# A planned instruction order for a linear-attention and SwiGLU block: priorities tuned wait by wait, one product moved, six idle products and eight ordering edges added

## The chip, the cores and the metric

The kernel runs on one core of one Trainium2 chip. The metric is the device time of one execution in microseconds (us), taken as the median of several executions.

## The reference

The input x has 2048 rows of 1024 values. The reference computes, with all matrices in bf16:

```python
xn = layernorm(x)
q, k, v = split(xn @ wqkv)                 # 32 heads of 32
pq, pk = phi(q), phi(k)                    # phi(t) = (t+1 if t > 0 else exp(t)) + 1e-6
kv = einsum("bhsd,bhse->bhde", pk, v); z = pk summed over s
s = (pq @ kv / (pq . z + 1e-6)) @ wo
g = silu((silu(x @ w_gate) * (x @ w_up)) @ w_down)    # w_gate, w_up: 1024 x 3584
out = x + s * g
```

Here x in the second branch is the layernormed xn as well.

## The kernel before

**Products.** Most matrix products are cut as in Strassen's method: a 2 x 2 block product is made from seven products of sums and differences of blocks (numbered 1 to 7 in the code) instead of eight. Where the products 1 and 5 belong to two neighbouring column blocks, they are cut once more (the "joint" products, named j1a to j1d and j5a to j5d). VectorE (DVE) makes the sums of weight blocks and of data blocks, ScalarE (ACT) copies results out of the eight PSUM banks, and DVE adds intermediate sums back into a bank. A product 6 of a set is followed by such an addition (`ps <- ps, TM`), and product 7 of that set writes into the bank that the addition reads, so it has to wait for it.

**Stages.** First K and V for all 16 row tiles (each tile is normalised by `ln_tile`, turned on its side by `t_tile`, and multiplied by `p_piece` for the first two tiles, by sets for the others; `a_tile` sums up kv). `combos` (line 523) makes four differences of weight blocks for K and V in two DVE instructions each. Then two passes over half of the rows: queries, gate and up products, the attention output, and last the down projection (`down`), whose order of products is written out in the strings `IN_D`, `ON_D`, `OUT_D` and `END_D`. `OUT_D` holds for the end of the first pass alone. The mark `X` in it calls `turn_pass`, which loads the second half of the data into the arena P, makes its differences, and prepares the first query pair of the second pass.

**Order.** The text of the kernel only lists operations with what they read and write. The class `Plan` decides on the order in which each engine runs them. `place` is a list scheduler on planned costs: it walks through time and gives each engine the next operation. TensorE (PE) takes the oldest ready group among the next six of the written order (`WINDOW=6`); DVE, ACT, GpSimd (POOL) and SyncE (SP, all DMA issues but two) take the ready one with the earliest due time less its `boost`. Due times (`schedule`) are counted back from the written order of PE's work. `schedule` runs `place` 24 times; between two runs `lift` (line 138) adds 2.0 to the boost of operations that were held up on a chain that made PE wait by 0.15 or more, and the plan with the earliest end is kept. `emit` turns the plan into one instruction list for each engine with semaphore waits. Each engine then runs its list strictly in that order, so an instruction that waits holds up everything behind it on its engine.

**The start.** Two loads of x tiles and four loads of 512 KB of K weights are issued in a row. PE runs 15 warm-up products on zeros (`NWARM`), then the transposes of tile 0 (four groups of two), then the K product of tile 0, one load of weights at a time. In `ln_tile` the DVE instructions of one tile are: two statistics, one aggregation (line 744), `veps` (line 745), then POOL raises it to the power -1/2 (`rstd`, line 748), then for tiles 0 and 1 two DVE instructions normalise a half each (line 755). The list `first` holds operations of tile 0 that the statistics of tile 1 have to follow.

Of the kernel before, what the change touches and what calls it, by code (L numbers as in the profile page):

```python
# [10 lines left out]
ALU = mybir.AluOpType  # L11
# [4 lines left out]
GRAN = 256  # L16


PASSES, LIFT = 24, 2.0
TABLE, DMA_SLACK, HOLD, YIELD = 1.28, 2.0, 0.1, 10  # L20


# [12 lines left out]
class Plan:  # L35
# [71 lines left out]
    def schedule(self):  # L107
        ops = self.ops
        for o in reversed(ops):
            d = o.pecum if o.eng == "pe" else o.pecum + o.cushion  # L110
            for s in o.succs:
                extra = (4.0 + o.nbytes / 200e3) if o.sem is not None else o.busy + o.lat
                d = min(d, s.dl - extra)
            o.dl = d - o.urgent
        pes = [o for o in ops if o.eng == "pe"]
        cum = [o.pecum + o.busy for o in pes]
        for o in ops:
            if o.sem is not None and o.succs:
                k = bisect_right(cum, o.dl - self.lead) - 1
                if k >= 0 and pes[k] not in o.preds:  # L120
                    o.preds.add(pes[k])
                    pes[k].succs.append(o)
        best = None
        for n in range(PASSES):
            end = self.place()
            if best is None or end < best[0] - 0.01:
                best = (end, self.order, {o: (o.start, o.done) for o in ops})
            if n + 1 < PASSES:
                self.lift()
        self.order = best[1]  # L130
        for o, (a, b) in best[2].items():
            o.start, o.done = a, b
        return self.order

    def lift(self):

        prev, last = {}, {}
        for o in self.order:
            prev[o] = last.get(o.eng)
            last[o.eng] = o  # L140
        for o in self.order:
            p = prev[o]
            if o.eng != "pe" or p is None or o.start - p.start - p.busy < 0.15:
                continue
            c = o
            for _ in range(12):
                late = max(c.preds, key=lambda p: p.done, default=None)
                if late is None:
                    break
                if c.eng not in ("pe", "sp") and c.start - max(c.ready, late.done) > 0.02:  # L150
                    c.boost += LIFT
                c = late

    def place(self):
        ops = self.ops
        for o in ops:
            o.npred = len(o.preds) + len(o.after)
            o.ready = 0.0
        free = {e: 0.0 for e in self.ENGS}
        dma_free = 0.0  # L160
        tab = None
        avail = {e: [] for e in self.ENGS}
        pe_next = deque(o for o in ops if o.eng == "pe")
        for o in ops:
            if o.npred == 0:
                avail[o.eng].append(o)
        order = []
        done = set()
        total = len(ops)
        while len(order) < total:  # L170
            best = None
            for e in self.ENGS:
                a = avail[e]
                if not a:
                    continue
                t = free[e]
                if e == "pe":
                    lim = None
                    n = 0
                    for o in pe_next:  # L180
                        if n >= self.window:
                            lim = o.idx
                            break
                        n += 1
                    cand = [o for o in a if lim is None or o.idx < lim]
                    if not cand:
                        continue
                    rdy = [o for o in cand if o.ready <= t + 0.05]
                    o = min(rdy, key=lambda o: o.idx) if rdy else min(cand, key=lambda o: (o.ready, o.idx))
                else:  # L190
                    rdy = [o for o in a if o.ready <= t]
                    soon = [o for o in a if o.ready > t]
                    while rdy:
                        o = min(rdy, key=lambda o: (o.dl - o.boost, o.idx))
                        q = [q for q in soon if q.ready + HOLD < t + o.busy and q.dl - q.boost + YIELD < o.dl - o.boost] if e != "sp" else ()
                        if not q:
                            break
                        rdy.remove(o)
                    if not rdy:
                        o = min(soon or a, key=lambda o: (o.ready, o.dl))  # L200
                s = max(t, o.ready)
                if e == "act" and o.tab is not None and o.tab != tab:
                    s += TABLE
                if best is None or s < best[0]:
                    best = (s, e, o)
            s, e, o = best
            if o.tab is not None:
                tab = o.tab
            o.start = s
            if o.sem is not None:  # L210
                free[e] = s + o.busy
                b = max(s + 1.8, dma_free)
                dma_free = b + o.nbytes / 340e3
                o.done = dma_free + DMA_SLACK
            else:
                free[e] = s + o.busy
                o.done = s + o.busy + o.lat
            avail[e].remove(o)
            if e == "pe":
                done.add(o)  # L220
                while pe_next and pe_next[0] in done:
                    pe_next.popleft()
            order.append(o)
            for q in o.succs:
                q.npred -= 1
                q.ready = max(q.ready, s + o.busy if q.eng == o.eng and (o.eng == "pe" or o in q.after) else o.done)
                if q.npred == 0:
                    avail[q.eng].append(q)
        self.order = order
        return max(o.done for o in ops)  # L230

    def emit(self, esem):
        prog = {e: [] for e in self.ENGS}
# [55 lines left out]
def build_kernel(nc, A_x, A_wqkv, A_wo, B_w_gate, B_w_up, B_w_down, out, WINDOW=6, NWARM=15, NPE=4, LEAD=12.0):  # L289
# [12 lines left out]
    with ExitStack() as es:  # L302
# [24 lines left out]
        X = Arena("X", 28 * KB)  # L327
# [24 lines left out]
        ps = [es.enter_context(nc.psum_tensor("ps%d" % b, [128, 512], F32)) for b in range(8)]  # L352
        bank_r = [named("bank", b) for b in range(8)]
# [36 lines left out]
        PL = Plan(WINDOW, LEAD)  # L390
# [6 lines left out]
        def pe_mm(reads, writes, mms):  # L397
            return PL.op("pe", reads, writes, partial(_mm_group, mms), mm_cost(mms))
# [21 lines left out]
        def tt(reads, writes, o, a, b, op, fast=False):  # L420
            return dve(reads, writes, lambda h: h.tensor_tensor(o, a, b, op), nel(o), 1.92 if fast else 0.96)  # L421
# [98 lines left out]
                                          ("R10", PQ0 + 8 * KB), ("R11", PQ0 + 12 * KB), ("T2", RB0),  # L520
                                          ("T3", RB0 + 4 * KB), ("T4", RB0 + 8 * KB))}

        def combos(v):
            for o, a, b in (("T3", "R11", "R01"), ("T1", "R01", "R00"), ("T2", "R11", "T1"), ("T4", "R10", "T2")):
                for h in range(2):
                    w = {}
                    for nm in (o, a, b):
                        ap, r = v[nm]
                        n = len(r.keys) // 2
                        w[nm] = ap[:, 2 * h:2 * h + 2, :], Region(r.keys[n * h:n * h + n])  # L530
                    tt([w[a][1], w[b][1]], [w[o][1]], w[o][0], w[a][0], w[b][0], ALU.subtract, True)


        wz = TM.at(0, 1 * KB, FP16)
# [3 lines left out]
        for n in range(NWARM):  # L538
            b = n % 8
# [193 lines left out]
        def ln_tile(i):  # L733
# [18 lines left out]
            if i < 2:  # L752
                n = 512
                for c in range(0, 1024, n):
                    o0 = dve([s.r, mvr, rsr], [o.sub(2 * c, 2 * n).r], lambda h, c=c: h.tensor_scalar(
                        oa[:, c:c + n], xa[:, c:c + n], mv[:, j, 0:1], rstd[:, j, :], ALU.subtract, ALU.mult), n, 2.6)
                if i == 0:
                    first.append(o0)
            else:
                dve([mvr, rsr], [nmr], lambda h: h.scalar_tensor_tensor(  # L760
                    nmean[:, j, :], mv[:, j, 0:1], -1.0, rstd[:, j, :], ALU.mult, ALU.mult), 60)
                act([s.r, nmr, rsr], [o.r], oa, xa, ACT.Identity, "sb", bias=nmean[:, j, :], scale=rstd[:, j, :])
# [152 lines left out]
                o.urgent = 60.0 - 2 * n  # L915
        ln_tile(0)
        t_tile(0)
        ln_tile(1)
        p_piece(0, 0, 1)
        p_piece(0, 0, 0)  # L920
# [5 lines left out]
        ln_tile(2)  # L926
        p_piece(0, 1, 1)
        t_tile(2)
        combos(KVV[0])
        p_piece(1, 1, 1)  # L930
        ln_tile(3)
        p_piece(0, 1, 0)
# [638 lines left out]

        IN_D = "7_0 3_0 7_1 3_1 H nj1a 4_0 nj1b 4_1 nj1c n2_0p nj1d n2_0q nj5a n2_1p nj5b n2_1q nj5c n6_0 nj5d"
        ON_D = "L 7_0 K0 6_1 7_1 K1 nj1a 3_0 nj1b 3_1 S nj1c 4a nj5a nj1d 4b nj5b n2_0 nj5c n2_1 nj5d n6_0"
        OUT_D = "7_0 3_0 X 6_1 7_1 nj1a 3_1 nj1b nj1c 4a nj5a nj1d 4b nj5b n2_0 nj5c n6_0 n2_1 nj5d n6_1"
        END_D = "7_0 6_1 7_1 3_0 3_1 4_0 4_1"

        def down(p):
# [171 lines left out]
```

## Time and profile before

| what | value |
|---|---|
| median of 4 runs | 717.62 us (716.91 to 718.32) |
| profiled execution, its own time | 716.91 us |
| its span, first to last instruction | 715.2 us |
| PE busy | 707.1 us, 99% |
| DVE busy | 641.8 us, 90% |
| ACT busy | 405.5 us, 57% |
| mean granted TensorE clock | 0.999 |

A row of the timeline gives the start and the length in us, engine, line, operation, what is written and read, how many instructions are merged into the row, and in brackets the idle time before them with what ended it. PE is the matmul stream, PEld the loading of its stationary operand, which runs beside it. The end of a matmul is modelled, so two matmuls that follow each other closely overlap in such rows; the spacing of starts tells more.

### The profile page before, as it was taken

To read this page: it belongs to the slowest core of one execution; us is meant where nothing else is said; L and a number is where in the kernel's file an instruction comes from. 1 tells how busy PE (TensorE), PEld (TensorE's weight loads), DVE (VectorE), ACT (ScalarE), POOL (GpSimd) and SP (SyncE) were. 2 spreads that over 40 slices of the span, in tenths; PEclk is the share of its full clock that TensorE was granted. 3 is DMA by queue.
4 is the path that set the end of the run, shared out by engine and by line. 5 is a ranking of instruction groups with operands and counts; after the bars stand their busy time and mean duration, and the time that the engine had idled before them with its cause. 6 is when DMAs were issued, how large, how long until landed. Compare 5 with 4: busy or idle time off the path is not lost.

```text
span 715.2 us, 11264 instructions
## 1 busy us (share of the span) xinstructions
PE 707.1 (99%) x4143; PEld 389.4 (54%) x4143; DVE 641.8 (90%) x1533; ACT 405.5 (57%) x779; POOL 12.8 (2%) x35
## 2 busy tenths in 40 slices
PE   8999999999999999999999999999999999999997
PEld 3544445555555555555556455555555555565654
DVE  6999888989999999998957999999999999797863
ACT  3767654887669565654222157676886756521212
POOL 2111000000000000000000000000000000000000
PEclk9999999999999999999999999999999999999999
DMA  9425235145464343326595964132715241646653
GB/s 298 114 60 127 51 117 177 60 141 198 143 191 121 125 143 124 97 73 168 145 196 159 275 161 141 60 118 93 206 61 179 87 148 60 180 137 160 143 155 96
DMA packets 138758, 98.11 MB, mean 137 GB/s; under 512 B 32848, under 2 KB 135760, under 8 KB 138704
## 3 DMA queue, kind: packets, MB, share of 16 engines
q1 hardware_dynamic: 138416, 97.21, 47.8%
q8 instruction: 32, 0.52, 0.3%
q10 hardware_dynamic: 288, 0.20, 0.1%
q14 instruction: 22, 0.18, 0.1%
HBM read 77.59 MB, written 12.71 MB: 126 GB/s over the span
## 4 chain that ended last, share of the span: by engine, by line
PE 95%; DVE 2%; DMA 1%; ACT 0%; SPq 0%; issue 0%
PE ps L278 95%; DMA H<-in_A_wqkv_dram 1%; DVE W L421 1%; DVE H L421 1%; DVE ps L421 0%; PE ps L285 0%; DVE TM L421 0%; DVE P L421 0%; ACT TM L410 0%; SPq L424 0%; ACT ps L410 0%; DVE H L818 0%; SPq L722 0%; DVE TM L817 0%; DVE X L421 0%
## 5 line engine op out<-in xcount | busy, mean ns | idle before, releaser
L278 PE MATMUL ps<-X,W 128*128 128x512 f16 (+2 forms) x1372 | 289.2, 350 | 0.6 <-DVE W L421 0.6
L410 ACT ACTIVATE TM<-ps 128x512 f16<-128x512 f32 (+3 forms) x355 | 186.8, 548 | 108.9 <-PE ps L278 106.5
L278 PE MATMUL ps<-H,W 128*128 128x512 f16 (+2 forms) x1096 | 219.2, 351 | 0.6 <-DVE ps L421 0.4
L421 DVE TENSOR_TENSOR W<-W 128x1024 f16<-128x1024 bf16 (+5 forms) x416 | 186.4, 482 | 6.0 <-PE ps L278 5.2
L278 PEld LDWEIGHTS ps<-X,W 128*128 128x128 f16 (+1 forms) x1372 | 132.6, 98 | 105.0 <-DVE W L421 1.1
L278 PEld LDWEIGHTS ps<-H,W 128*128 128x128 f16 (+1 forms) x1096 | 105.5, 98 | 95.2 <-DVE ps L421 1.5
L421 DVE TENSOR_TENSOR ps<-ps,TM 128x256 f32<-128x256 f32 (+1 forms) x250 | 131.4, 529 | 13.2 <-PE ps L278 10.9
L410 ACT ACTIVATE ps<-ps 128x512 f32<-128x512 f32 (+1 forms) x174 | 85.1, 489 | 100.1 <-PE ps L278 98.3
L278 PE MATMUL ps<-P,W 128*128 128x256 f16 (+1 forms) x516 | 99.5, 319 | 0.1
L410 ACT ACTIVATE H<-ps 128x512 f16<-128x512 f32 (+1 forms) x126 | 75.1, 605 | 41.5 <-PE ps L278 41.3
L421 DVE TENSOR_TENSOR H<-H 128x1024 f16<-128x1024 f16 (+5 forms) x126 | 70.7, 580 | 1.3 <-DMA H<-in_A_wqkv_dram 0.8
L278 PEld LDWEIGHTS ps<-P,W 128*128 128x128 f16 (+1 forms) x516 | 50.3, 98 | 29.5 <-DVE ps L421 0.7
L410 ACT ACTIVATE TM<-TM 128x512 f16<-128x512 f32 (+1 forms) x61 | 37.9, 622 | 47.0 <-DVE TM L421 46.7
L278 PE MATMUL ps<-W 128*128 128x256 f16 (+1 forms) x330 | 62.0, 282 | 0.0
L421 DVE TENSOR_TENSOR TM<-ps,TM 128x512 f32<-128x512 f32 (+3 forms) x63 | 41.7, 662 | 13.2 <-PE ps L278 12.4
L421 DVE TENSOR_TENSOR H<-H,TM 128x512 f16<-128x512 f16 x112 | 45.6, 419 | 8.9 <-ACT H L410 8.7
L278 PEld LDWEIGHTS ps<-W 128*128 128x128 f16 (+1 forms) x330 | 31.6, 98 | 32.5 <-DVE ps L421 1.3
L278 PE MATMUL ps<-H,X 128*128 128x512 bf16 (+1 forms) x150 | 35.5, 379 | 0.8 <-DMA H<-in_A_wqkv_dram 0.8
L278 PE MATMUL ps<-H,P 128*128 128x512 bf16 (+1 forms) x110 | 26.8, 379 | 0.0
L421 DVE TENSOR_TENSOR H<-ps,TM 128x512 f16<-128x512 f32 (+1 forms) x35 | 24.0, 687 | 1.9 <-PE ps L278 1.5
L278 PEld LDWEIGHTS ps<-H,X 128*128 128x128 f16 (+1 forms) x150 | 14.0, 98 | 17.9 <-ACT X L410 1.2
L421 DVE TENSOR_TENSOR TM<-TM,W 128x512 f16<-128x512 f16 (+1 forms) x39 | 14.2, 366 | 10.5 <-ACT TM L410 10.5
(97 smaller groups left out, 431.3 us busy)
## 6 DMA issues: line engine op xcount, KB each, us to landing
W<-in_B_w_gate_dram SPq DMA_DIRECT2D x14, 1024.0 KB, 5.2
W<-in_B_w_up_dram SPq DMA_DIRECT2D x13, 1024.0 KB, 5.5
W<-in_B_w_down_dram SPq DMA_DIRECT2D x14, 896.0 KB, 6.3
H<-in_A_wqkv_dram SPq DMA_DIRECT2D x8, 512.0 KB, 8.0
H<-r_scratch SPq DMA_DIRECT2D x32, 128.0 KB, 3.6
W<-m_scratch SPq DMA_DIRECT2D x4, 1024.0 KB, 5.2
s_scratch<-TM SPq DMA_DIRECT2D x32, 128.0 KB, 2.5
TM<-in_A_x_dram SPq DMA_DIRECT2D x16, 256.0 KB, 3.4
```

Source lines behind the costliest of these rows:

```text
L278: last = h.matmul(o, l, r, start=st, stop=sp, skip_group_check=True)
L410: q = PL.op("act", reads, writes, lambda h: h.activation(o, i, func, **kw), nel(o) / (1000.0 if "bias" in kw or not isinstance(kw.get("sca ...
L421: return dve(reads, writes, lambda h: h.tensor_tensor(o, a, b, op), nel(o), 1.92 if fast else 0.96)
```

## The change

The planner's `lift` with its 24 passes goes. In its place `tune` plans once, takes the first place in order of time where PE's planned wait is over 0.1 us, collects up to 14 operations of ACT, DVE and POOL on the chain that led there which were held up by their own engine, and tries up to 24 variants: for the first one, two, three or all of them, their boost is raised, or that of the operation ahead of them lowered, by 2, 5 or 12. A variant counts by PE's planned idle time from the start up to 7 us of PE work beyond that place; the best is kept if it saves more than 0.03 us, otherwise the search goes on behind the place. `place` returns PE's idle time instead of the end, and can stop early.

Three edits change what is planned. Six products of 128 columns on zeros stand between the transposes of tile 0 and its first K product. The eight differences of K weight blocks have to follow the last normalising instruction of tile 1. In `OUT_D` product 6 of set 1 (`6_1`) stands first.

```diff
-PASSES, LIFT = 24, 2.0
+GAP, SPAN = 0.1, 7
...
-        best = None
-        for n in range(PASSES):
-            end = self.place()
...
+        self.tune()
+        self.place()
         return self.order
...
+    def tune(self):
+        self.place()
+        front = 0.0
+        while True:
+            prev, last, work, at = {}, {}, 0.0, None
+            for o in self.order:
+                p = prev[o] = last.get(o.eng)
+                last[o.eng] = o
+                if o.eng == "pe":
+                    if p is not None and work > front and o.start - p.start - p.busy > GAP:
+                        at = o
+                        break
+                    work += o.busy
+            if at is None:
+                return
+            held = []
+            c = at
+            for _ in range(14):
+                late = max(c.preds, key=lambda p: (p.done, p.idx), default=None)
+                if late is None:
+                    break
+                if c.eng in ("act", "dve", "pool") and c.start - max(c.ready, late.done) > 0.02:
+                    held.append((c, prev[c]))
+                c = late
+            base = self.place(work + SPAN)
+            best = None
+            for deep in (1, 2, 3, 14):
+                for lift in (2.0, 5.0, 12.0):
+                    for sign in (0, 1):
+                        part = held[:deep]
...
+                        for c, b in part:
+                            if sign and b is not None:
+                                b.boost -= lift
+                            else:
+                                c.boost += lift
+                        v = self.place(work + SPAN)
...
+            if best is not None and best[0] < base - 0.03:
+                for o, x in best[1]:
+                    o.boost = x
+            else:
+                front = work + 0.01
+            self.place()
...
             if e == "pe":
+                idle += s - was
+                work += o.busy
+                if work > limit:
+                    return idle
...
-        return max(o.done for o in ops)
+        return idle
...
-        def combos(v):
+        def combos(v, after=None):
...
-                    tt([w[a][1], w[b][1]], [w[o][1]], w[o][0], w[a][0], w[b][0], ALU.subtract, True)
+                    q = tt([w[a][1], w[b][1]], [w[o][1]], w[o][0], w[a][0], w[b][0], ALU.subtract, True)
+                    if after is not None:
+                        q.preds.add(after)
+                        after.succs.append(q)
...
-                if i == 0:
-                    first.append(o0)
+                first.append(o0)
...
         t_tile(0)
+        tr = [o for o in PL.ops if o.eng == "pe"][-1]
+        for n in range(6):
+            o = pe_mm(wz_r[:1], [bank_r[kvb[2]]], [(ps[kvb[2]][:, 0:128], wz[:, 0:128], wz[:, 0:128], True, True)])
+            o.preds.add(tr)
+            tr.succs.append(o)
+            o.urgent = -4.0
         ln_tile(1)
...
-        combos(KVV[0])
+        combos(KVV[0], first[-1])
...
-        OUT_D = "7_0 3_0 X 6_1 7_1 nj1a 3_1 nj1b nj1c 4a nj5a nj1d 4b nj5b n2_0 nj5c n6_0 n2_1 nj5d n6_1"
+        OUT_D = "6_1 7_0 3_0 X 7_1 nj1a 3_1 nj1b nj1c 4a nj5a nj1d 4b nj5b n2_0 nj5c n6_0 n2_1 nj5d n6_1"
```

More of the change, by code (lines that the diff above doesn't have):

```diff
@@ L122, in schedule @@
                     pes[k].succs.append(o)
-        best = None
-        for n in range(PASSES):
-            end = self.place()
[L126 to L132, printed above, removed]
-        return self.order
[L135 to L147, printed above, removed]
+        self.tune()
@@ L148, in lift @@
                 if late is None:
                     break
-                if c.eng not in ("pe", "sp") and c.start - max(c.ready, late.done) > 0.02:
-                    c.boost += LIFT
+                if c.eng in ("act", "dve", "pool") and c.start - max(c.ready, late.done) > 0.02:
+                    held.append((c, prev[c]))
                 c = late
-    def place(self):
+            base = self.place(work + SPAN)
[4 more added lines that the diff above has]
+                        part = held[:deep]
+                        if deep > 1 and len(held) < deep and deep != 14:
+                            continue
+                        old = [(o, o.boost) for c, b in part for o in (c, b) if o is not None]
+                        for c, b in part:
[4 more added lines that the diff above has]
+                        v = self.place(work + SPAN)
+                        new = [(o, o.boost) for o, _ in old]
+                        for o, x in reversed(old):
+                            o.boost = x
+                        if best is None or v < best[0]:
+                            best = (v, new)
@@ L155, in place @@
+            if best is not None and best[0] < base - 0.03:
+                for o, x in best[1]:
+                    o.boost = x
+            else:
+                front = work + 0.01
+            self.place()
+    def place(self, limit=1e9):
         ops = self.ops
+        idle = work = 0.0
         for o in ops:
@@ L209, in place @@
             o.start = s
+            was = free[e]
             if o.sem is not None:
```

## The prediction

> **What bounds the kernel now.** I read the page's busy shares first, then PE's groups by shape to count its products, then PE's timeline for spacings, then the full timeline around each hole.
>
> ```profile
> PE 707.1 (99%) x4143; PEld 389.4 (54%) x4143; DVE 641.8 (90%) x1533; ACT 405.5 (57%) x779; POOL 12.8 (2%) x35
> ```
>
> PE's busy time is modelled, so I count instead. In the row of 32 products below, each costs (7.08 - 0.38) / 31 = 0.216 us; 256 columns cost 0.109, 128 columns 0.056. The groups by shape add up to 2485, 1450 and 208 products of these widths: 536.3 + 158.3 + 11.7 = 706.3 us, less 5.0 because the 64 small products with Zh run side by side (32 of them in 0.99 us): 701.3. From PE's first product at 1.04 to its last end at 712.16 are 711.1 us. So some 9.6 us are waits, and this change can win from nothing else. By spacing they lie so: 1.4 in the warm-up, where products of 512 columns start every 0.427 us; 3.0 from there to 11.6 us (half of it before the first transpose); 3.1 in sixteen holes of 0.07 to 0.76 us in the rest; 0.8 before the very last transpose; about 1 in crumbs under 0.06.
>
> The start, from the timeline:
>
> ```profile
> 7.28 1.04 PE L278 MATMUL ps<-H,X 128*128 128x512 bf16 x4
> 7.55 0.21 DVE L744 BATCH_NORM_AGGREGATE mv<-stats 128x2 f32<-128x12 f32 x1
> 8.57 0.69 DVE L421 TENSOR_TENSOR H<-H 128x1024 f16<-128x1024 bf16 x1 [0.81 <-DMA H<-in_A_wqkv_dram]
> 8.69 1.02 PE L278 MATMUL ps<-H,X 128*128 128x512 bf16 x4 [0.37 <-DMA H<-in_A_wqkv_dram]
> 9.18 0.15 DVE L745 TENSOR_SCALAR veps<-mv 128x1 f32<-128x1 f32 x1
> 9.41 0.93 POOL L748 TENSOR_TENSOR rstd<-veps,neg_half 128x1 f32<-128x1 f32 x1 [3.39 <-DVE veps L745]
> 10.11 1.04 PE L278 MATMUL ps<-H,X 128*128 128x512 bf16 x4 [0.40 <-DMA H<-in_A_wqkv_dram]
> 10.37 0.73 DVE L755 TENSOR_SCALAR W<-W,mv,rstd 128x512 f16<-128x512 bf16 x2 [0.45 <-POOL rstd L748]
> ```
> ```profile
> 10.98 0.61 PE L285 MATMUL ps<-ident,W 128*128 128x128 f16 x8
> 11.58 7.08 PE L278 MATMUL ps<-H,X 128*128 128x512 bf16 x32
> ```
>
> The reader sees PE fed by one weight load each 1.4 us, and DVE's queue blocked: the weight difference at 8.57 waits for a landing, with tile 1's `veps`, ready at 7.8, behind it.
>
> The two largest holes lie after the pass turns (PE alone first, then all engines):
>
> ```profile
> 390.96 12.25 PE L278 MATMUL ps<-H,W 128*128 128x512 f16 x56
> 403.04 0.38 PE L278 MATMUL ps<-P,X 128*128 128x256 f16 x2
> 403.26 0.38 PE L278 MATMUL ps<-P,W 128*128 128x256 f16 x2
> 404.00 0.82 PE L278 MATMUL ps<-H,W 128*128 128x512 f16 x3 [0.36 <-DVE ps L421]
> ```
> ```profile
> 398.71 0.69 DVE L421 TENSOR_TENSOR TM<-ps,TM 128x512 f32<-128x512 f32 x1
> ...
> 403.24 0.70 DVE L421 TENSOR_TENSOR ps<-ps,TM 128x512 f32<-128x512 f32 x1
> ```
> ```profile
> 432.48 0.69 DVE L818 SCALAR_TENSOR_TENSOR H<-ps,TM 128x512 bf16<-128x512 f32 x1
> ...
> 433.28 0.69 DVE L421 TENSOR_TENSOR ps<-ps,TM 128x512 f32<-128x512 f32 x1
> ...
> 433.88 1.28 DVE L421 TENSOR_TENSOR W<-W 128x1024 f16<-128x1024 bf16 x2
> 434.62 0.55 PEld L278 LDWEIGHTS ps<-X,W 128*128 128x128 f16 x4 [1.09 <-DVE W L421]
> ```
> And DVE in stretches, from the windows table (PE, PEld, DVE, ACT, POOL):
>
> ```profile
> 332.00:342.00 10.00, 9.95 (x73) 6.60 (x71) 9.91 (x23) 3.33 (x8) 0.00 (x0) 1.00 0.36 98
> 440.00:460.00 20.00, 20.00 (x118) 11.33 (x116) 20.00 (x51) 13.74 (x28) 0.00 (x0) 1.00 0.27 86
> ```
>
> DVE is full for long stretches: a better order there shifts work and makes no room.
>
> **A rule that speaks against the change.** These waits count in full only if 0.216 us is PE's own pace. The Trainium skill, TensorE: Matmul & The Clock Gate, section Back-to-back issue gap, gives about 131 ns a product of 512 columns in streams of load and matmul. By it the wide products would need 326 us instead of 536, PE would have 210 us to spare, and removing its waits would be worth nothing. The row of 32, whose 0.098 us weight loads lie wholly beside the matmuls, says 0.216, and so do all long stretches. I take the row.
>
> **Part 1, six idle products.** The last transpose of tile 0 starts at 7.02, so PE is free at 7.08; the K product starts at 7.28, when ACT has copied the transposed tile. Six products of 0.056 take 0.34, to 7.42: the K product starts 0.14 later. Its four products then end at 8.28, and the next load lets PE go on at 8.69: cost 0. Without that load wait it would be 0.14. Gain: the first K products already run at 0.216, so there is no slow clock to prevent; 0 here, though another execution might come out of the warm-up later. Bounds -0.3 to +0.14; I take 0.
>
> **Part 2, weight differences behind tile 1's normalising.** Two differences (0.69 and 0.68) leave the front of DVE's queue. `veps` follows the aggregation by 0.25, as in tile 0: 7.80. In tile 0 the normalising starts 0.83 after `veps` (5.22 to 6.05), with POOL's power at 0.56. At 9.41 the power took 0.93, beside a DVE difference of two SBUF operands. The Trainium skill, SBUF — State Buffer, section SBUF: two separate sides, says that such a DVE instruction and a GpSimd one exclude each other for their whole length. By the row alone I would keep 0.93 (normalising at 9.0); by the rule, with the difference gone, 0.56 (8.63). Either is early enough: transposes can start 0.47 after it (6.05 to 6.52), at 9.5 or 9.1, and PE's second four K products end at 8.69 + 0.86 = 9.55. So the transposes (0.45) fill 9.55 to 10.00, in the hole of 0.56 before 10.11. The next four products end at 10.97. Before, PE had 0.56 + 0.16 of waits between 9.55 and 11.58. After: 0.11 before 10.11, and then either tile 1's products on weights already landed, ready when ACT has copied the tile (about 11.1, ACT being taken from 9.74 to 10.34), or a wait for the fourth load at 11.5. Gain 0.05 to 0.61; I take 0.45, the plan knowing both times. The differences run after 9.4, in DVE's old idle stretches (0.45 at 9.93, 0.52 at 11.1); their first users come after 24 us. Cover gone, it would be the 1.37 us of both. No DMA is added or moved.
>
> **Part 3, `6_1` first in `OUT_D`.** The 56 products are four sets of 14 (3.02 us each). PE may look six groups ahead, and the evacuations date them: 6_0 to 393.98, the first half of 6_1 while the addition for 6_0 runs, 7_0 until 398.5 (its addition at 398.71), 3_0, then the second half of 6_1, until 403.04. Its addition starts at 403.24, and 7_1 needs its bank: only four small products (0.44) cover 0.96. Written first, both halves of 6_1 follow 6_0 and the addition starts about 397.2, with 6 us of cover. Gain 0.52. Its operand is there: DVE makes the W differences of that set from 391.37 on, a pair of 0.6 each, before 393.98. What is late next: the addition (0.6 net) now stands ahead of the differences of P that the joint product at 403.04 reads; that one had no wait, and 7_1 can go first. One bank is held 6 us longer. The set's own follower, two W instructions at 403.85 and after, may move with it. No queue of SP or POOL is passed, except that issues whose due times count from there keep their order to PE's work. Bounds 0.2 to 0.52; I take 0.5.
>
> **Part 4, the tuned priorities.** They reorder DVE, ACT, POOL, and with them SP. Planned costs are near the trace: a 1024-wide DVE difference 0.60 planned, 0.60 spacing; 512-wide addition 0.60 and 0.60; ACT copy 0.48 and 0.50. So a plan without a hole should mean a run nearly without. By place:
> - 434.62, 0.76: the W sums at 433.88 stand behind an evacuation and an addition, and DVE idled 0.28 at 431.8. Moving one sum (0.60) forward is enough; late next are the evacuation and its bank. 0 to 0.76, I take 0.55.
> - 238.80 to 251.8, 0.09 + 0.34 + 0.10: a handover through one ACT copy of 0.59 with 0.22 of PE work beside it. 0 to 0.53, I take 0.3.
> - Down projection of both passes (338 to 341, 633 to 637, each 0.36; 353.05 and 648.53, each 0.19), 1.10: DVE is full (9.91 of 10). I take 0.45.
> - The rest, 0.22 in three holes of under 0.1, below what `tune` looks at: 0.1. The last transpose (0.84): the multiply ahead of it stands behind a residual addition of 0.4 of which 0.1 is felt: 0.05.
> - New holes where the trace shows none: the 24 old passes' boosts are gone, and `tune` sees 7 us only. 0 to 3; nearest row, a hole of 0.2 to 0.3: I take 0.25.
>
> Sum: 0.45 + 0.5 + 0.55 + 0.3 + 0.45 + 0.1 + 0.05 - 0.25 = 2.15. The profiled execution took 716.91 (its span 715.2 and 1.7 around it); the median of the runs is 0.7 higher, and the sum is taken off the median: 717.6 - 2.2 = 715.4.
>
> **Rivals.** (a) DVE stays the limit: where it is full, each moved instruction makes another late, and only parts 2 and 3 survive: 717.6 - 0.95 + 0.2 = 716.9. For it: the full stretches, and that holes of 0.2 stand exactly there. Against: the largest holes come from queue order. The same time comes out if `tune` finds nothing that helps. (b) Slower: a DVE instruction that reads a landing is lifted to the front of DVE's list at the pass turn. DVE's order is fixed, so it blocks as at 8.57, and as DVE is full until 460, PE pays one for one. The loads P<-x_scratch take 2.6 to 9.0 us to land; the plan's formula gives a load of 512 KB 5.3. A lift on the slow one would cost 3.7: 717.6 - 1.4 + 3.7 = 719.9. It decides from a lateness of 2.9 on. Against: before, no DVE wait on a landing beyond 0.4 us shows after the start.
>
> **Numbers.** No change means within 0.2%, 1.4 us, about what a measurement can tell. Main case 0.69 (713.5 to 716.2), (a) 0.20 (716.2 to 718.3), (b) 0.11 (over 719.1). Faster 0.70, same 0.19, slower 0.11. All holes closed would give 717.6 - 3.1 - 0.6 - 0.3 = 713.6; the range runs from there to 717.7, leaving out (b) and the end of (a).
>
> **What would show it.** Tile 1's transposes near 9.6 with POOL's power at 0.56; no hole at 404; the W sums before 433; PE's spacing sum under 8 us. I am wrong if holes of 0.3 or more stand at new places, or a DVE row shows a DMA wait after 380.

## The result, and the profile after

The changed kernel takes 716.41 us (median of 35 runs, 715.19 to 717.21), the kernel before 717.57 (median of 55 runs): 1.2 us less, a ratio of 0.9982 with a 95% interval of 0.9977 to 0.9987. The profiled execution of it took 716.58, span 714.8. The direction was as forecast, the size about half of the 2.2 us that I had summed up: the saving is clear of the noise, but lies within the 1.4 us that I had called no change.

The page's busy shares, and the windows table of the two stretches shown of before (PE, PEld, DVE, ACT, POOL). Source lines lie 31 to 39 further down than before, so L278 is now L309, L421 is L452.

```profile
PE 707.6 (99%) x4149; PEld 390.7 (55%) x4149; DVE 641.7 (90%) x1533; ACT 404.4 (57%) x779; POOL 12.5 (2%) x35
```
```profile
332.00:342.00 10.00, 10.00 (x75) 7.03 (x74) 9.75 (x23) 3.62 (x7) 0.00 (x0) 1.00 0.32 88
440.00:460.00 20.00, 20.00 (x118) 11.32 (x116) 20.00 (x54) 14.02 (x28) 0.00 (x0) 1.00 0.25 79
```

PE has its six products more, DVE the same work. Where DVE was full it had enough room for another order: PE has no hole (a start of a product that comes later than the one before it needs) left at 338 to 341. The holes at 238 to 252 are gone too. The largest of them, in the profile before (two products of 256 columns need 0.22 us, so the row at 239.37 comes about 0.35 late):

```profile
238.80 0.39 PE L278 MATMUL ps<-H,TM 128*128 128x256 f16 x2
239.37 0.82 PE L278 MATMUL ps<-H,W 128*128 128x512 f16 x3 [0.17 <-ACT ps L410]
```

The start, from the timeline of all engines:

```profile
7.01 0.50 PE L309 MATMUL ps<-TM 128*128 128x128 f16 x6
7.73 0.15 DVE L779 TENSOR_SCALAR veps<-mv 128x1 f32<-128x1 f32 x1
7.88 1.02 PE L309 MATMUL ps<-H,X 128*128 128x512 bf16 x4 [0.37 <-DMA H<-in_A_wqkv_dram]
7.96 0.55 POOL L782 TENSOR_TENSOR rstd<-veps,neg_half 128x1 f32<-128x1 f32 x1 [2.01 <-DVE veps L779]
8.55 0.73 DVE L789 TENSOR_SCALAR W<-W,mv,rstd 128x512 f16<-128x512 bf16 x2 [0.67 <-POOL rstd L782]
9.37 1.02 PE L309 MATMUL ps<-H,X 128*128 128x512 bf16 x4 [0.46 <-DMA H<-in_A_wqkv_dram]
10.23 0.39 PE L316 MATMUL ps<-ident,W 128*128 128x128 f16 x4
10.78 1.04 PE L309 MATMUL ps<-H,X 128*128 128x512 bf16 x4 [0.17 <-DMA H<-in_A_wqkv_dram]
11.66 0.39 PE L316 MATMUL ps<-ident,W 128*128 128x128 f16 x4
12.27 1.90 PE L309 MATMUL ps<-H,X 128*128 128x512 bf16 x8 [0.23 <-DMA H<-in_A_wqkv_dram]
```

DVE's part went as drawn: `veps` straight behind the aggregation, the power 0.55 instead of 0.93, the normalising at 8.55. PE got nothing out of it. Its two halves of tile 1's transposes stand between sets of four K products, and the last set still waits for the fourth load. That load landed at 12.22 here and at 11.54 in the profile before, though it was issued at the same time (3.28 and 3.30). So the later profile began with a handicap of 0.7 us.

At 404 PE now runs through, and the DVE addition that made the hole there starts at 398.14 instead of 403.24:

```profile
398.14 0.69 DVE L452 TENSOR_TENSOR ps<-ps,TM 128x512 f32<-128x512 f32 x1
402.21 2.97 PE L309 MATMUL ps<-H,W 128*128 128x512 f16 x13
```

The largest new hole, and what is left of the pass turn, from the same timeline:

```profile
26.15 2.36 ACT L441 ACTIVATE W<-W,nmean,rstd 128x1024 f16<-128x1024 bf16 x2
28.41 1.08 ACT L441 ACTIVATE TM<-ps 128x512 f32<-128x512 f32 x2
29.37 0.61 ACT L441 ACTIVATE ps<-ps 128x512 f32<-128x512 f32 x1
30.03 1.04 PE L309 MATMUL ps<-H,X 128*128 128x512 bf16 x4 [0.60 <-ACT ps L441]
```
```profile
433.14 2.20 PE L309 MATMUL ps<-X,W 128*128 128x512 f16 x8
435.18 1.03 PE L309 MATMUL ps<-P,W 128*128 128x512 f16 x4
436.04 1.03 PE L309 MATMUL ps<-X,W 128*128 128x512 f16 x4
436.90 0.38 PE L309 MATMUL ps<-P,X 128*128 128x256 f16 x2
437.71 0.61 PE L309 MATMUL ps<-P,W 128*128 128x256 f16 x3 [0.42 <-DVE W L452]
```

At 30 us two normalising activations of ACT (2.36 us) stand ahead of the copy that PE needs. Eight products need 8 x 0.216 + 0.163 = 1.89 us in such a row; 2.20 hides a hole of 0.30 at 434. At 437.71 PE starts 0.59 later than 436.90 + 2 x 0.109. Before, there was one hole of 0.76 here, at 434.62; now there are two with 0.89 together.

**One yardstick.** The time of a profiled execution here is always PE's last end plus 4.75 to 4.78 us (716.91 - 712.16; 716.58 - 711.83). In every one of these kernels PE waits for the landing of the fourth K load and goes on 0.04 to 0.05 us after it; behind it, the two programs that were profiled twice repeat themselves to 0.02 and 0.11 us. So I use the difference "PE's last end less the landing of the fourth K load", both read from the trace. A hole is a start-to-start spacing of PE beyond what the first of the two products needs (0.216, 0.109 or 0.056); where a matmul's record is missing from a trace its 0.216 is taken off.

| kernel | ratio to before (95%) | profiled, us | 4th load landed | PE's last end | difference |
|---|---|---|---|---|---|
| before | 1 | 716.91 | 11.54 | 712.16 | 700.62 |
| before, again (e5) | one run | 717.07 | 11.71 | 712.31 | 700.60 |
| changed | 0.9982 (0.9977 to 0.9987) | 716.58 | 12.22 | 711.83 | 699.61 |
| changed, again (e6) | one run | 716.12 | 11.64 | 711.37 | 699.72 |
| new planner alone (e1) | 0.9986 (0.9977 to 0.9995) | 716.85 | 12.46 | 712.07 | 699.61 |
| the three edits, old planner (e7) | 1.0004 (0.9995 to 1.0014) | 717.53 | 11.68 | 712.75 | 701.08 |
| changed, no edge (e2) | 0.9983 (0.9974 to 0.9992) | 717.57 | 12.91 | 712.82 | 699.91 |
| changed, no idle products (e9) | 0.9985 (0.9976 to 0.9994) | 716.93 | 11.81 | 712.18 | 700.37 |
| changed, old `OUT_D` (e10) | 0.9982 (0.9973 to 0.9991) | 717.19 | 12.59 | 712.43 | 699.84 |
| changed, query load first (e12) | 0.9990 (0.9981 to 0.9999) | 716.30 | 11.78 | 711.54 | 699.76 |
| changed, swap at the start (e3) | 0.9978 (0.9969 to 0.9987) | 716.13 | 12.63 | 711.38 | 698.75 |
| changed, window 10 (e4) | 0.9983 (0.9974 to 0.9991) | 717.30 | 13.32 | 712.53 | 699.21 |
| changed, swap, window 11 (e11) | 0.9965 (0.9951 to 0.9979) | 715.00 | 11.10 | 710.24 | 699.14 |

Ratios of single steps overlap; the differences and the holes are what tells steps of 0.3 us apart. Apart from those of before and changed, each difference rests on one profile.

### The profile page after: what moved, and what is told of

The parts are those of the page before. It is cut to its first block, busy times and chain, and to the rows that moved or that the text cites. A ratio compares the mean times of both kernels' runs of the same rounds, so it can differ in the third digit from the quotient of the medians.

```text
span 714.8 us, 11277 instructions
## 1 busy us (share of the span) xinstructions
PE 707.6 (99%) x4149; PEld 390.7 (55%) x4149; DVE 641.7 (90%) x1533; ACT 404.4 (57%) x779; POOL 12.5 (2%) x35
## 4 chain that ended last, share of the span: by engine, by line
PE 94%; DVE 2%; ACT 2%; DMA 1%; SPq 0%; issue 0%
PE ps L309 94%; DMA H<-in_A_wqkv_dram 1%; ACT TM L441 1%; DVE ps L452 0%; DVE H L851 0%; DVE W L452 0%; ACT W L441 0%; DVE TM L452 0%; DVE H L1035 0%; SPq L455 0%; ACT ps L441 0%; ACT L441 0%; DVE TM L850 0%; PE ps L316 0%; ACT X L441 0%
## 5 line engine op out<-in xcount | busy, mean ns | idle before, releaser
L309 PE MATMUL ps<-X,W 128*128 128x512 f16 (+2 forms) x1372 | 289.2, 350 | 0.1
L309 PE MATMUL ps<-H,W 128*128 128x512 f16 (+2 forms) x1096 | 218.9, 351 | 0.1
L452 DVE TENSOR_TENSOR W<-W 128x1024 f16<-128x1024 bf16 (+5 forms) x416 | 186.4, 482 | 6.1 <-PE ps L309 5.3
L309 PEld LDWEIGHTS ps<-X,W 128*128 128x128 f16 (+1 forms) x1372 | 132.7, 98 | 103.8 <-DVE ps L452 0.8
L309 PEld LDWEIGHTS ps<-H,W 128*128 128x128 f16 (+1 forms) x1096 | 106.1, 98 | 95.1 <-DVE ps L452 0.6
L452 DVE TENSOR_TENSOR ps<-ps,TM 128x256 f32<-128x256 f32 (+1 forms) x250 | 131.7, 529 | 12.6 <-PE ps L309 10.2
L309 PE MATMUL ps<-P,W 128*128 128x256 f16 (+1 forms) x516 | 99.8, 319 | 0.4 <-DVE W L452 0.4
L452 DVE TENSOR_TENSOR H<-H 128x1024 f16<-128x1024 f16 (+5 forms) x126 | 71.4, 581 | 0.6 <-ACT H L441 0.4
L309 PEld LDWEIGHTS ps<-P,W 128*128 128x128 f16 (+1 forms) x516 | 50.3, 98 | 29.7 <-DVE W L452 0.7
L309 PE MATMUL ps<-W 128*128 128x256 f16 (+1 forms) x330 | 61.6, 282 | 0.1
L452 DVE TENSOR_TENSOR TM<-ps,TM 128x512 f32<-128x512 f32 (+3 forms) x63 | 41.7, 662 | 13.0 <-PE ps L309 12.3
L452 DVE TENSOR_TENSOR H<-H,TM 128x512 f16<-128x512 f16 x112 | 45.3, 418 | 8.4 <-ACT H L441 8.1
L309 PEld LDWEIGHTS ps<-W 128*128 128x128 f16 (+1 forms) x330 | 31.7, 98 | 31.9 <-DVE ps L452 1.9
L309 PE MATMUL ps<-H,X 128*128 128x512 bf16 (+1 forms) x150 | 35.7, 379 | 1.8 <-DMA H<-in_A_wqkv_dram 1.2
L309 PE MATMUL ps<-H,P 128*128 128x512 bf16 (+1 forms) x110 | 26.8, 379 | 0.0
L452 DVE TENSOR_TENSOR H<-ps,TM 128x512 f16<-128x512 f32 (+1 forms) x35 | 24.1, 688 | 2.6 <-PE ps L309 2.1
L309 PEld LDWEIGHTS ps<-H,X 128*128 128x128 f16 (+1 forms) x150 | 14.0, 98 | 18.4 <-ACT ps L441 1.1
L452 DVE TENSOR_TENSOR TM<-TM,W 128x512 f16<-128x512 f16 (+1 forms) x39 | 14.2, 366 | 10.5 <-ACT TM L441 10.5
```

The source lines that it names most:

```text
L309: last = h.matmul(o, l, r, start=st, stop=sp, skip_group_check=True)
```

## The experiments

**e5 and e6: the same two programs once more.**

> The kernel before, unchanged, profiled once more. My theory: the first 12 us hang on the landing of the fourth K weight load (11.54 in the first profile, issued at 3.30), which differs between executions of one program by over 1 us, while the rest of the kernel repeats to within 0.1 us. So the time from that landing to PE's last end is again 700.6 (712.16 - 11.54), whatever the landing is. Rival (other parts vary too, for instance the warm-up's clock or DVE): that difference moves by more than 0.3.

> The changed kernel, unchanged, profiled once more. My theory: from the landing of the fourth K weight load to PE's last end again 699.6 (711.83 - 12.22), and the same holes: 0.76 at 30, 0.25 at 133, 0.30 at 434, 0.59 at 438. Rival (the holes at 434 and 438 depend on when a store lands): these two move by over 0.2.

Measured: differences 700.60 and 699.72, against 700.62 and 699.61. All sixteen holes of before are there again, to 0.01; those of the changed kernel too (0.76, 0.25, 0.29, 0.59), with a new one of 0.11 at 411. The first theory holds for before; for the changed kernel one place is not steady (see e12). The change is worth 0.9 to 1.0 us by this measure, in line with 1.2 by the medians; the two first profiles show only 0.3 because of the landings.

**e1 and e7: planner and edits apart.**

```diff
 e1: before, with schedule/tune/place of the changed kernel
 e7: the changed kernel, with
-GAP, SPAN = 0.1, 7
+PASSES, LIFT = 24, 2.0
 and schedule/lift/place of before
```

> The kernel before with the new planner (tune) alone: no idle products, no ordering edge on the weight differences, old OUT_D. My theory: the holes add up one by one. The holes of 0.1 to 0.3 at 238 to 252, 338 to 341 and 633 to 637 are gone (1.25 in all), the one of 0.5 at 404 is still there, and after the second turn of the pass there are still waits of about 0.8 at 434; a new hole of up to 1 us stands within the first 40 us. Median 0.7 below before: 716.9, ratio 0.9990. Rival (the tuned order alone carries the whole change): 716.4, ratio 0.9982. Rival (DVE is the limit, holes only move): 717.6, ratio 1.000.

> The three written edits (idle products, edge, OUT_D) with the old planner of 24 passes. My theory: the edits bring nothing by themselves; the old planner deals new holes, the largest about 1.4 us near 30 and 1 us near 548: median 717.6 to 718.3, ratio 1.000 to 1.001. Rival (what I predicted for parts 2 and 3): 0.95 below before, 716.6.

Measured: the planner alone has the same difference as the whole change (699.61), ratio 0.9986; the edits alone 701.08, ratio 1.0004, so nothing. In e1 the holes of 238 to 252, 338 to 341 and 633 to 637 are gone, as expected, 404 still has its 0.52, and there is a new hole of 0.61 at 19; but 434 and 438 have only 0.53 together, less than I had said. The rival of e1, that the tuned order carries the whole change, is the right one by the difference; the interval of the ratio holds both 0.9990 and 0.9982. In e7 the hole at 404 is gone and 434 falls to 0.12, but the old planner deals two new holes of 1.0, at 30 and at 548, which eat it up. The second, from PE's timeline:

```profile
547.96 0.39 PE L278 MATMUL ps<-H,TM 128*128 128x256 f16 x2 [0.85 <-DVE TM L421]
```

All ten programs with the tuner lie between 698.75 and 700.43 (e8, below, the highest), both with the old planner at 700.60 or above. But the ten differ among themselves by more than the change is worth. A plan placed once, with neither `lift` nor `tune`, was not run, so how much of the gain the search has earned, and how much another order would have brought by chance, is open.

**e2: no edge.**

```diff
-        combos(KVV[0], first[-1])
+        combos(KVV[0])
```

> The changed kernel without the edge that puts the K weight differences behind tile 1's normalising. My theory: the start is tied to the landing of the fourth K weight load, so the transposes of tile 1 are late again (after the third set of four K products) and cost nothing there; only the hole that the tuned order leaves between 15 and 40 us changes its place. Median 0.0 to 0.3 above the changed kernel: 716.4 to 716.7. Rival (what I predicted for this part): early transposes fill a hole, so without the edge 0.45 more: 716.9, and the PE waits between the first transposes and 13 us grow by 0.45.

Measured: 699.91. Tile 1's transposes run behind the third set of four again, and PE goes on right after the fourth landing, as with the edge. The hole of 0.76 at 30 gives way to one of 0.60 at 20, and 412 has 0.55. The cost of 0.45 at the start that the rival expected is not there: PE goes on 0.05 us after the landing with and without the edge. Further on the edge seems to cost something: without its hole at 412 (see e12) e2 would stand at 699.36, 0.25 below the changed kernel.

**e3: swap at the start.**

```diff
         p_piece(0, 0, 1)
-        p_piece(0, 0, 0)
         t_tile(1)
         p_piece(1, 0, 1)
+        p_piece(0, 0, 0)
```

> The changed kernel with one more edit: in the written order, tile 1's transposes and its K product on the first two weight loads come ahead of tile 0's K product on the last two loads. My theory: the order of PE's products kept the gain of the early transposes away, since each set of four was queued ahead of work that was ready. Now PE has tile 1's product to run while it waits for loads three and four: PE waits from the first transposes to 15 us fall by 0.3 to 0.6, and the hole of 0.76 at 30 us, which belongs to the same plan, falls to about 0.15: median 715.5 to 716.0, ratio to before 0.997 to 0.998. Rival (the loads or DVE set the pace of the start, whatever the order): 716.4, the waits reappear before 25 us.

Measured: 698.75, ratio 0.9978. The hole at 30 is gone and no other came before 133. But the start did not fill, which my theory wanted. From the timeline:

```profile
10.55 0.61 PE L316 MATMUL ps<-ident,W 128*128 128x128 f16 x8
11.17 1.04 PE L309 MATMUL ps<-H,X 128*128 128x512 bf16 x4
11.24 0.59 ACT L441 ACTIVATE X<-ps 128x512 f16<-128x512 f16 x1
12.90 0.81 PE L309 MATMUL ps<-H,X 128*128 128x512 bf16 x3 [0.69 <-DMA H<-in_A_wqkv_dram]
```

Tile 1 is copied by 11.83, and PE stands still from 12.03 to 12.68 (one record is missing before 12.90) for the load that lands at 12.63. The set of four that needs this load is next in PE's list; as the planner takes the oldest group that is ready, it must have counted on an earlier landing. So both sides missed: the waits at the start did not fall, and yet the kernel gained 0.9, all of it behind the landing and most of it by losing the hole at 30. The edge alone does not make that hole, since e3 has the edge. But it has a share: all seven profiles with the edge, a window of six and the written start (both of the changed kernel, e7, e8, e9, e10, e12) have a hole of 0.76, or 1.03 with the old planner, at 29.5 to 30.4, and none without the edge has one there. By what path, no run shows.

**e9: no idle products.**

```diff
-        for n in range(6):
-            o = pe_mm(wz_r[:1], [bank_r[kvb[2]]], [...])
```

> The changed kernel without the six idle products. My theory: they lie in a wait for the first K weight load, and no K product ran slow before: the time from the landing of the fourth K load to PE's last end is 699.6 to 699.7 as with them; median 716.4. Rival (they keep PE's clock up): the first K products start at 0.43 us spacing instead of 0.216, and PE is up to 0.3 later.

Measured: 700.37, with a hole of 0.76 at 412; without that hole 699.61, as in the changed kernel. The first K products run at 0.216 without the idle products (four in a row of 1.02 us at 7.47), so these are worth nothing in this execution. Nor in e5, which has no idle products and whose warm-up products all ran at 0.427 to the end: its K products start every 0.216 all the same. The rival falls, as far as these 14 profiles go.

**e10: the old `OUT_D`.**

```diff
-        OUT_D = "6_1 7_0 3_0 X 7_1 nj1a ..."
+        OUT_D = "7_0 3_0 X 6_1 7_1 nj1a ..."
```

> The changed kernel with the old OUT_D. My theory: the hole of 0.52 at 404 is back, and the waits at 434 and 438 shrink by about as much as in the run of the tuned order alone (0.89 to 0.53), since what is due after the pass turn is late anyway: from the landing of the fourth K load to PE's last end 699.7 to 699.9; median 716.5. Rival (what I predicted for part 3): 0.5 later, 716.9.

Measured: 699.84. From PE's timeline around 404 and 434:

```profile
404.30 0.38 PE L309 MATMUL ps<-P,W 128*128 128x256 f16 x2
405.04 1.25 PE L309 MATMUL ps<-H,W 128*128 128x512 f16 x5 [0.36 <-DVE ps L452]
```
```profile
435.27 1.04 PE L309 MATMUL ps<-X,W 128*128 128x512 f16 x4 [0.20 <-DVE ps L452]
...
437.87 0.38 PE L309 MATMUL ps<-P,X 128*128 128x256 f16 x2
438.25 1.04 PE L309 MATMUL ps<-P,W 128*128 128x256 f16 x5
```

The 0.52 is back (405.04 against 404.30 + 0.22), and 434 and 438 have 0.36 + 0.16 instead of 0.30 + 0.59. Moving `6_1` takes 0.52 away and gives 0.37 back 30 us later; the difference moves by 0.23 (by 0.12 against the second profile of the changed kernel, which has the hole of 0.11 at 411), as the first theory said, not by 0.5.

**e12: the query weights' load first.** DVE's list reads the weights X (1 MB) for the second pass around 395 to 397. From e9's timelines of DVE and of PE:

```profile
396.49 0.69 DVE L452 TENSOR_TENSOR X<-X 128x1024 f16<-128x1024 bf16 x1 [0.84 <-DMA X<-in_A_wqkv_dram]
```
```profile
410.21 1.03 PE L309 MATMUL ps<-W 128*128 128x512 f16 x4
411.83 0.39 PE L309 MATMUL ps<-W 128*128 128x256 f16 x2 [0.60 <-DVE ps L452]
```

DVE blocks for 0.84 us and is then busy without a break (7.99 to 8.00 of the 8 us from 406 to 414 in the changed kernel's two profiles and in e2's), until PE has a hole of 411.83 - 410.21 - 0.86 = 0.76. The pairs of DVE wait and hole at 411 to 413, over the runs with the tuner and `6_1` first (e8, whose order differs here, and e12 apart), are: 0 and 0 (e3), 0 and 0 (changed), 0.18 and 0.11 (e6), 0.27 and 0.21 (e4), 0.50 and 0.44 (e11), 0.61 and 0.55 (e2), 0.84 and 0.76 (e9). The hole is the wait less 0.06 to 0.08. (e7, whose order is the old planner's, waits 0.30 there and shows no hole.)

Neither before, nor e1, nor e10, all with the old `OUT_D`, shows this DVE wait. That is not because they read X later. In the profile before, the sum stands at the same place of DVE's list:

```profile
395.32 0.69 DVE L421 TENSOR_TENSOR X<-X 128x1024 f16<-128x1024 bf16 x1
```

In all profiles but those of e8 and e12, DVE is ready for this sum 8.14 to 8.15 us after the load was issued (387.18 here). The load itself takes from 7.73 us (before) to 9.04 (e9). So the old order ran the same race, and won it by 0.41 in before and by only 0.02 in e1 and e10. The load took 7.73 to 8.16 in the four profiles with the old `OUT_D` and 7.90 to 9.04 in the eight with `6_1` first, so the new order may slow it as well; the changed kernel alone has 7.90 and 8.38, and no run separates this. What `OUT_D` does change is DVE's slack behind the sum. From the windows tables of e10 and of the changed kernel (DVE is the third of the engines):

```profile
401.00:412.00 11.00, 10.64 (x55) 5.05 (x53) 10.54 (x27) 2.60 (x6) 0.00 (x0) 1.00 0.85 238
401.00:412.00 11.00, 11.00 (x59) 5.52 (x58) 10.99 (x31) 3.00 (x6) 0.00 (x0) 1.00 0.82 247
```

With the old order DVE idles 0.46 us there (0.16 in the profile before) and could catch up, which no run puts to the test; with the new one it idles 0.01.

```diff
             pump(1)
+            for o in PL.ops[k:]:        # k: number of operations ahead of pump
+                if o.sem is not None:
+                    o.urgent = 20.0
```

> The changed kernel with the load of the next pass's query weights (X, 1 MB) issued ahead of the 512 KB load of P that stood before it. My theory: the holes of 0.1 to 0.8 at 412, in the kernels with 6_1 first, come from this load: DVE's list reaches its first sum at 395.5, and where the load lands later DVE blocks, and PE pays that less 0.07 us sixteen us later. Issued 0.5 us earlier and with 512 KB less before it, it lands near 394: no DVE wait for it and no hole at 412. From the landing of the fourth K load to PE's last end 699.4 to 699.7, median 716.2. Rival (the hole comes from DVE being full, whatever the load does): a hole of 0.1 or more between 408 and 425 stays, or moves to the P load (DVE waiting for x_scratch).

Measured: 699.76. The load was issued at 387.26 and landed at 395.08, 0.67 earlier than in the changed kernel and not near 394. The planner put DVE's sum earlier as well, and DVE waited 0.92; the holes are 0.38 at 412 and 0.21 at 419, together less than the wait by 0.33 and not by 0.07, and the one of 0.59 at 438 is gone. My remedy fails, and a hole between 408 and 425 stayed, which is what the rival expected; but DVE again waited for the load, so the run does not decide between the two. In favour of the load stand the two profiles of the changed kernel: they are of one program, and the hole at 411 is in the one that has the wait. A list is only as good as the landing times it counts on.

**e4, e8 and e11: more reach for PE, less for DVE.**

```diff
 e4:  WINDOW=6 -> WINDOW=10
 e8:  turn_dma() adds x only if (p, self.h) != (0, 1)
 e11: the edit of e3 and WINDOW=11
```

> The changed kernel with PE choosing among ten written groups instead of six. Theory A: after the pass turn the waits (0.30 at 434 and 0.59 at 438) stand because every group within reach waits for DVE or ACT; with ten in reach PE finds one, and both shrink to under 0.3 together, as do the waits of 0.19 at 354 and 648: median 1.0 below the changed kernel, 715.4. Theory B (DVE is full there and has to be caught up with at some point): the waits move to a later place by 445 and the time stays at 716.4.

> The changed kernel without the seven DVE additions of x to the last quarter of the first pass (0.42 us each, about 3 us of DVE work between 410 and 437; that quarter of the output then lacks s * g). Theory A (DVE is the limit after the pass turn): the waits of 0.30 at 434 and 0.59 at 438 shrink to under 0.3 together. Theory B (the order, a bank or a store's landing makes them): they stay at 0.7 to 0.9. The other holes stay as in the changed kernel either way. Median 716.4 less what goes: 715.7 by A, 716.3 by B.

> Both edits that helped, together: tile 1's products first (swap) and PE choosing among eleven written groups. My theory: the gains add up, since they are at different places (start and 30 us: 0.86; pass turn: 0.4 to 0.8): from the landing of the fourth K load to PE's last end 698.0 to 698.5; median 715.2 to 715.6, ratio to before 0.9965 to 0.9975. Rival (the tuned plan deals new holes whenever something changes): 699 and 716.2.

Measured: e4 699.21. The holes at 434 and 438 shrink from 0.89 to 0.07, plus 0.20 at 443, and those of 0.19 at 354 and 648 are gone, as theory A has it; the hole of 0.76 at 30 is one of 0.16 at 36, as the plan is another; 0.56 in small holes at 229 to 260, 0.16 at 524 and 0.21 at 413 are new. So PE had other work to do after the pass turn, beyond the sixth group, as far as one plan can be compared with another. In the ratio (0.9983) no gain shows.

e8, which leaves out eight additions and not seven (ratio 0.9987, 0.9977 to 0.9996, difference 700.43) settles nothing: with less DVE work the plan came out different everywhere there. 434 and 438 fall to 0.39, but DVE and ACT wait for DMAs and PE has 0.72 and 0.51 at 423 and 424. Whether DVE's load or its order made the hole at 434 is left open.

e11 is the fastest kernel measured, 715.31 us and 0.9965, but its two gains do not add up: 699.14 is within 0.1 of e4 and 0.4 worse than e3, with a hole of 0.44 at 410. By the difference the rival is right (699), by the median of 715.31 my theory. Its five runs all fell between 715.0 and 715.71; the one profiled had the earliest landing of all (11.10). How much of its ratio the order has earned, and how much early landings, these runs do not tell. By the difference, e3 is the best.

## Why the prediction was right in direction and too large in size

- **The time and the signs.** 716.41 lies just outside the band of the main case (to 716.2) and in that of rival (a), but not by (a)'s cause: it is the tuned order that survived, not parts 2 and 3. Of my signs of being wrong both came: a hole of 0.76 at a new place, and a DVE wait for a DMA after 380 (0.18 at 395.68 in e6). Of my signs for it, 404 and the power of 0.55 came; the waits between PE's first product and its last end fell from 9.8 us (I had put 9.6, and my list of them adds up to 9.3) to 9.2, not under 8. The terms missed both ways, by about 1.9 us downwards (the holes at 434 and 438, the new ones, part 2) and 0.6 upwards; that half of the sum came out is in part luck.
- **PE is the bound, and only its waits count.** Right. The 0.216 us held in every kernel; by the 131 ns of the Trainium skill, TensorE: Matmul & The Clock Gate, section Back-to-back issue gap, which I had set aside, the whole change would have been worth nothing. The holes behind the fourth landing (the last transpose's included) fell from 3.97 to 3.25 us, and the difference by 0.9 to 1.0; the rest is in crumbs under 0.06.
- **Part 1, 0.** Right (e9): in all 14 profiles the fast spacing set in ahead of the first K product.
- **Part 2, taken at 0.45, measured 0.05 or less.** The working up to the transposes was right, and so was the power: 0.55 without the DVE difference beside it, 0.93 with it, in line with the rule of exclusion that I had cited. The step that failed is the choice between "tile 1's products" and "a wait for the fourth load": it is the wait. I had the bound of 0.05 and took the other end for "the plan knowing both times". The plan does not know them: the same load, issued at the same time, landed between 11.10 and 13.32. And the edge has a share in the new hole at 30 (e2, e3), which I had put at nothing.
- **Part 3, taken at 0.5, measured 0.23 net, less what a late load costs.** The hole at 404 went, as worked out from the four sets. What failed is "what is late next", which I gave nothing: 434 and 438 lose 0.37 of it again, and DVE has no slack left behind the sum that reads X, so that a late landing costs PE 0 to 0.76.
- **Part 4, term by term.** 434.62: taken 0.55; together with 438 it is 0.76 to 0.53 under the tuner alone (0.23), and 0.76 to 0.89 with `OUT_D`. 238 to 252: taken 0.3, got all 0.53. Down projection: taken 0.45 of 1.10, got 0.72; DVE being 99% busy was no obstacle there. Three small ones: taken 0.1, got nothing. Last transpose: 0.05 taken, 0.10 got. **New holes: taken 0.25, measured 1.0 (0.76 at 30 and 0.25 at 133).** Of all terms this one was mis-sized most: I priced it at one small hole. Both new holes stand where the kernel before had none over 0.08.
- **Rivals.** (a), DVE as the limit, was wrong at 338 to 341, where DVE was busy for 9.91 of 10 us; after the pass turn a wait that was taken away came back, and whether DVE's load or its order did that is open (e8). (b) came true in a small size and at the place named: DVE blocked on a landing at the pass turn, up to 0.84 us (0.92 in e12) and not 3.7, with PE paying almost one for one in five profiles. But no instruction had been lifted to the front for it: the sum stands where it stood in the kernel before, and the load came later. I had put the point of decision at 2.9 and so gave its smaller sizes no term in the sum.

## What to carry to other kernels

Where the busiest engine is already 99% busy, add up its holes by spacing, and for each fix write down what becomes late next with a number, not with zero. Judge steps of 0.3 us by a landmark inside the trace that comes after the noisy part (here the landing of the fourth load), not by the time of one execution. A static order takes transfer times for granted; each transfer that it reads just in time is a bet. Look at how much a landing moves between executions, and at how much the engine that waits for it idles afterwards: that idle time is what can take a late landing up.

## What the runs showed of the hardware that I had not expected

- The first 512 KB load, issued at 1.71 to 1.75 us in each execution, landed between 6.59 and 8.82. The next three followed every 1.5 us, but for the second one in e6, e7 and e12, which took 1.8 to 1.95. Over the executions in the table the fourth landing moves by as much, which alone moves the time by 2.2 us, more than the change. The traffic of the core's DMAs dips meanwhile, in each profile a little differently: in e2 it falls from about 390 GB/s at 3 us to 59 to 94 between 3.7 and 4.4. Why, no run shows.
- The granted clock reads 1.00 in the profile's rows while the warm-up products start every 0.427 us instead of 0.216; the faster spacing set in at 3.9 us at the earliest, and in three executions not before the warm-up's last product at 5.7. The rows miss it because the trace's record of the clock begins only with the change (4.02 in the profile before, 6.41 in that of the changed kernel, 6.82 in e5, the latest but still ahead of the first K product), and they count the time ahead of the record as full. PE's wait of 1.5 us just before the K products in e4 did not bring the slow spacing back.
